# When the rows of x are loaded and Wq is turned: one fused attention and FFN kernel, its DMA queue reordered

## Chip, cores, metric

One core of a Trainium2 chip. The metric is the device time of one execution in microseconds (us), the median of several runs. The profiled span is some 1.7 us shorter than the time of the same execution. The experiments ran on three chips, each beside runs of the kernel before on the same chip in the same rounds; so medians of different rounds compare only roughly.

## The reference, cut to what matters

```python
x = A_x                                      # [1, 2048, 640], bf16
h  = x + _A_ref(_layernorm(x), A_wqkv, A_w_phi, A_wo)      # 32 heads of 20
h2 = h + _B_ref(_layernorm(h), B_w_gate, B_w_up, B_w_down) # (x Wg * x Wu) Wd, F = 1536
# _A_ref: q, k, v = x @ wqkv; phi(k) = [softmax(k w_phi), softmax(-k w_phi)], phi(q) likewise
#         kv = phi(k)^T v; num = phi(q) kv; den = phi(q) sum(phi(k)); out = (num / den) @ wo
```

## The kernel before

The 2048 rows are 16 tiles of 128. In the first third of the kernel each tile is loaded, normalised (VectorE statistics, then `xn`), turned so that the model dimension lies on the partitions (`xt`), and multiplied with Wv and Wk (`V`, `K`); `KV` sums phi(k)^T v. Tiles 0 to 3 are turned on TensorE, all others by a DMA transpose ("row turn") on the SyncE queue. The weights that make phi(q) are folded into Wq once (`F0`); for that Wq itself is turned by five DMA transposes (`wqt0` to `wqt4`), and the first fold needs all five.

All instructions are nodes of a graph. A table gives each a place, a list scheduler turns the places into one fixed order per engine, and each engine's program waits on semaphores only for what its next instruction needs. So every engine runs strictly in its order: an instruction that waits holds up all that stand behind it.

```python
xload("sp", 6, 8, -91, also=["act"])            # the last of the rows loaded with the weights
...
PACE = {t: [] for t in range(NT)}               # PACE[t]: issued only behind the row turn of tile t
...
for j in range(4):                              # x8, x10, x12, x14: two tiles of rows each
    PACE[3 + j].append(xload("sp", 8 + 2 * j, 10 + 2 * j, 10 * (3 + j) - 19))
for g in range(NC):                             # the five turns of Wq
    PACE[7 + g // 2].append(wqt(g, 10 * (7 + g // 2) - 19))
...
else:                                           # tiles 4 to 15: turned by DMA
    G.op("sp", "xt%d" % t, ... e.dma_start_transpose(out=T["xnT"][...], in_=T["xn"][...]), ...)
    for o_ in PACE[t]:
        o_.before.append(G.by["xt%d" % t])
```

The order of the SyncE queue that comes out: `w5 x0 x2 wk4 wv2 x6 x8 | xt6 xt4 x10 xt7 wqt0 x14 wqt1 xt5 x12 | xt8 wqt2 xt9 wqt4 wqt3 xt11 ...`. The ScalarE queue issues `x1 wk0 wk2 wv0 x4 wv4` (`wk2` is Wk's second piece: two row blocks, 320 KB).

The softmax here doesn't subtract the row's maximum and nothing guards it: scores larger than these inputs give would overflow.

Of the kernel before, what the change touches and what calls it, by code (L numbers as in the profile page):

```python
# [47 lines left out]
x0:1.18 wk0:1.18:1 wk2:1.66:1 wk4:2.14 x1:0.7 wv0:2.14 wv2:2.62:1 wv4:3.1 x2:1.66:1 x4:2.62:1 x6:3.1 w5:0.7 x8:3.58 x10:20.107 x12:25.947 x14:23.027  # L48
wqt0:21.807 wqt1:23.507 wqt2:31.138 wqt3:34.798 wqt4:33.578 wo0:51.868 wo2:49.468 wg0:49.948 wu0:52.348 wg1:52.828 wu1:50.428 wg2:50.908 wu2:51.388
wg3:48.988 wu3:47.548 wg4:48.028 wu4:48.508 id0:1.97 gl0:1.72 eps:0.7 id1:3.81 gla0:3.59 glb0:4.21 gla4:2.49 glb4:5.105 gla1:2.27 glb1:3.15 gla2:2.71  # L50
glb2:3.37 gla3:2.93 glb3:4.885 va1:0.9 glx:6.134 kv1:6.534 zero:0.7 warm0:1.08 warm1:1.51 warm2:1.94 warm3:2.37 warm4:2.8 warm5:3.23 warm6:3.66
warm7:4.09 warm8:4.52 warm9:5.019 Ph0:4.58:1 Ph1:4.43 Ph2:5.475 WT0:4.74 WTe0:5.289 WT1:5.239 WTe1:6.377 WT2:7.119 WTe2:7.807:1 WT3:6.84 WTe3:7.389
WT4:10.022 WTe4:10.572 F1_0:6.284 Fe1_0:6.869:1 F1_1:7.398 Fe1_1:8.022 F1_2:8.406 Fe1_2:9.269:1 F1_3:7.987 Fe1_3:8.646 F1_4:11.405 Fe1_4:11.99:1
L1s0:5.557 L1a0:6.795 L1s1:3.027 L1a1:4.027 L1s2:9.552 L1a2:10.552 L1s3:8.732 L1a3:10.372 L1s4:10.708 L1a4:12.848 L1s5:11.528 L1a5:14.708 L1s6:12.958
L1a6:14.598 L1s7:13.778 L1a7:14.818 L1s8:16.167 L1a8:24.428 L1s9:15.347 L1a9:22.078 L1s10:23.608 L1a10:25.358 L1s11:24.538 L1a11:26.888 L1s12:33.398
L1a12:36.248 L1s13:31.158 L1a13:34.718 L1s14:36.468 L1a14:37.468 L1s15:28.418 L1a15:36.358 L1l0:7.492 L1e0:7.922 L1l1:4.317 L1e1:4.747 L1l2:11.195
L1e2:11.625 L1n2:11.935 L1n3:12.135 L1l4:15.196 L1e4:16.04 L1n4:16.75 L1n5:16.55 L1n6:16.35 L1n7:16.95 L1l8:27.397 L1e8:27.857 L1n8:28.659 L1n9:28.859
L1n10:33.777 L1n11:33.977 L1l12:38.281 L1e12:38.711 L1n12:41.254 L1n13:41.454 L1n14:41.654 L1n15:41.854 xn0:8.232 xt0:9.127 xte0:9.892 xn1:5.057
xt1:5.737 xte1:6.905:1 xn2:12.348 xt2:13.901 xte2:14.573 xn3:12.613:1 xt3:13.621 xte3:14.928:1 xn4:17.487 xt4:18.887 xn5:17.387:1 xt5:24.727 xn6:16.987
xt6:17.667 xn7:19.407 xt7:20.587 xn8:29.238 xt8:29.918 xn9:29.462:1 xt9:32.358 xn10:34.218 xt10:37.238 xn11:34.91:1 xt11:36.018 xn12:41.988 xt12:42.668  # L60
xn13:42.488 xt13:45.108 xn14:42.378:1 xt14:43.888 xn15:44.408 xt15:46.328 V0_0:10.845 V0_1:11.117 V0_2:12.535 V0_3:12.806 V0_4:13.078 Ve0:13.95
K0_0:14.18 K0_1:14.451 K0_2:14.723 K0_3:14.995 K0_4:15.266 Kx0_0:16.14 Kx0_1:18.1 Ks0:19.907 Kr0:21.865 Ke0:22.728 Kn0:23.552 KV0:26.405 V1_0:9.479
V1_1:9.751 V1_2:11.72 V1_3:11.992 V1_4:12.263 Ve1:13.326 K1_0:7.713 K1_1:8.856 K1_2:10.302 K1_3:10.573 K1_4:13.35 Kx1_0:15.416 Kx1_1:16.763 Ks1:17.987
Kr1:19.97 Ke1:20.833 Kn1:21.193 KV1:29.798 V2:15.538 Ve2:19.347 K2:19.613 Kx2_0:21.242 Kx2_1:22.105 Ks2:25.468 Kr2:27.617 Ke2:28.067 Kn2:29.059
KV2:31.832 V3:18.255 Ve3:21.327:1 K3:16.896 Kx3_0:18.723 Kx3_1:20.21 Ks3:22.188 Kr3:24.958 Ke3:25.94 Kn3:26.3 KV3:33.866 V4:27.081 Ve4:28.838 K4:23.688
Kx4_0:25.317 Kx4_1:26.15 Ks4:26.998 Kr4:28.598 Ke4:30.798 Kn4:31.418 KV4:37.259 V5:32.508 Ve5:34.136 K5:28.439 Kx5_0:30.175 Kx5_1:31.008 Ks5:31.978
Kr5:33.688 Ke5:34.76 Kn5:36.536 KV5:40.967 V6:22.33 Ve6:24.335 K6:20.972 Kx6_0:22.878 Kx6_1:23.712 Ks6:29.738 Kr6:31.632 Ke6:32.082 Kn6:34.177
KV6:41.643 V7:25.047 Ve7:26.773 K7:30.474 Kx7_0:32.232 Kx7_1:33.065 Ks7:34.828 Kr7:36.794 Ke7:38.501 Kn7:38.895 KV7:46.709 V8:35.901 Ve8:37.657
K8:34.542 Kx8_0:36.171 Kx8_1:37.034 Ks8:37.867 Kr8:39.467 Ke8:39.917 Kn8:42.054 KV8:48.743 V9:37.935 Ve9:39.563:1 K9:39.293 Kx9_0:40.922 Kx9_1:41.755
Ks9:42.988 Kr9:44.885 Ke9:45.335 Kn9:45.695 KV9:50.777 V10:42.634 Ve10:44.262 K10:43.992 Kx10_0:45.62 Kx10_1:46.454 Ks10:47.287 Kr10:48.887 Ke10:49.75  # L70
Kn10:50.11 KV10:54.17 V11:56.205 Ve11:58.045 K11:45.35 Kx11_0:47.077 Kx11_1:47.91 Ks11:48.744 Kr11:50.584 Ke11:51.034 Kn11:52.469 KV11:60.28 V12:49.419
Ve12:51.184 K12:47.385 Kx12_0:49.127 Kx12_1:49.96 Ks12:50.794 Kr12:52.394 Ke12:52.844 Kn12:54.828 KV12:61.271 V13:54.846 Ve13:56.588 K13:51.453
Kx13_0:53.082 Kx13_1:53.915 Ks13:54.748 Kr13:56.348 Ke13:57.212 Kn13:57.572 KV13:62.262 V14:58.922 Ve14:60.648 K14:52.812 Kx14_0:54.538 Kx14_1:55.372
Ks14:56.205 Kr14:57.805 Ke14:58.668 Kn14:59.931 KV14:62.938 V15:63.929 Ve15:65.557 K15:57.563 Kx15_0:59.192 Kx15_1:60.025 Ks15:60.858 Kr15:62.458
Ke15:62.908 Kn15:63.268 KV15:67.446 KVe0:68.392 KVe1:69.612 KVe2:69.002 F0_0:42.319 Fe0_0:43.092 F0_1:60.956 Fe0_1:61.541 F0_2:63.614 Fe0_2:64.199
F0_3:40.652 Fe0_3:41.237:1 F0_4:61.947 Fe0_4:62.532:1 Q0_0:66.366 Qx0_0_0:68.232 Qx0_0_1:67.716 Q0_1:68.122 Qx0_1_0:69.471 Qx0_1_1:69.987 Q0_2:70.28
Qx0_2_0:71.629 Qx0_2_1:72.146 Q0_3:65.287 Qx0_3_0:67.153 Qx0_3_1:66.636 Q0_4:69.201 Qx0_4_0:70.55 Qx0_4_1:71.067 Q1_0:90.865 Qx1_0_0:92.214
Qx1_0_1:92.731 Q1_1:82.062 Qx1_1_0:83.412 Qx1_1_1:83.928 Q1_2:85.579 Qx1_2_0:86.928 Qx1_2_1:87.445 Q1_3:80.638 Qx1_3_0:82.504 Qx1_3_1:81.987
Q1_4:79.559 Qx1_4_0:80.908 Qx1_4_1:81.425 Q2_0:72.783 Qx2_0_0:74.649 Qx2_0_1:74.132 Q2_1:89.441 Qx2_1_0:90.79 Qx2_1_1:91.307 Q2_2:71.359 Qx2_2_0:72.708
Qx2_2_1:73.225 Q2_3:74.552 Qx2_3_0:76.418 Qx2_3_1:75.902 Q2_4:88.017 Qx2_4_0:89.882 Qx2_4_1:89.366 Q3_0:76.711 Qx3_0_0:78.06 Qx3_0_1:78.577 Q3_1:83.142  # L80
Qx3_1_0:84.491 Qx3_1_1:85.007 Q3_2:78.48 Qx3_2_0:79.829 Qx3_2_1:80.346 Q3_3:91.944 Qx3_3_0:93.293 Qx3_3_1:93.81 Q3_4:75.632 Qx3_4_0:77.497
Qx3_4_1:76.981 wd0:94.253 wd1:94.733 wd2:93.773 wd3:93.293 N0_1:73.862 N0_0:74.207 sr0:74.477 rho0:74.967 A0:75.337 B0:76.367 dd0:77.397 rd0:77.787
o0:78.267 oT0:79.688 O0:84.221 h0:86.057 L2s0:87.108 L2a0:88.108 L2v0:88.559 L2r0:90.778 hc0:89.038:1 hT0:89.929 N1_1:77.79 N1_0:72.438 sr1:78.405
rho1:78.895 A1:79.265 B1:80.295 dd1:81.325 rd1:81.715 o1:82.195:1 oT1:83.107 O1:86.658 h1:88.287 L2s1:89.538 L2a1:90.668 L2v1:90.958 L2r1:91.648
hc1:90.958:1 hT1:91.638 N2_1:89.096 N2_0:90.52 sr2:90.358 rho2:91.458 A2:91.828 B2:92.858 dd2:93.888 rd2:94.278 o2:94.758 oT2:96.179 O2:103.403
h2:105.032 L2s2:105.993 L2a2:107.423 L2v2:108.564 L2r2:109.277 hc2:107.713 hT2:108.637 N3_1:81.717 N3_0:78.135 sr3:82.927 rho3:83.417 A3:83.787
B3:84.817 dd3:85.847 rd3:86.808 o3:87.288 oT3:88.709 O3:93.023 h3:94.652 L2s3:95.713 L2a3:96.723 L2v3:97.013 L2r3:97.753 hc3:97.883:1 hT3:98.563
N4_1:94.382 N4_0:94.727 sr4:95.403 rho4:96.533 A4:96.903 B4:98.383 dd4:99.585 rd4:100.147 o4:100.798:1 oT4:101.71 O4:109.818 h4:111.822 L2s4:112.925
L2a4:114.055 L2v4:114.345 L2r4:115.455 hc4:114.345 hT4:115.268 N5_1:106.198 N5_0:104.762 sr5:107.113 rho5:107.885 A5:108.427 B5:109.758 dd5:110.96
rd5:111.522 o5:112.002 oT5:113.423 O5:116.563 h5:118.192 L2s5:119.123 L2a5:120.123 L2v5:120.413 L2r5:120.913 hc5:120.413:1 hT5:121.093 N6_1:99.984  # L90
N6_0:100.329 sr6:101.53 rho6:102.355 A6:102.933 B6:104.135 dd6:105.783 rd6:106.813 o6:107.293 oT6:109.857 O6:121.182 h6:122.81 L2s6:123.872
L2a6:124.882 L2v6:125.172 L2r6:128.373 hc6:125.172 hT6:126.095 N7_1:135.035 N7_0:141.855 sr7:135.65 rho7:142.47 A7:142.84 B7:143.87 dd7:144.9
rd7:145.29 o7:145.77 oT7:147.191 O7:151.868 h7:153.525 L2s7:154.457 L2a7:156.028 L2v7:156.318 L2r7:157.528 hc7:157.028:1 hT7:157.708 N8_1:112.958
# [131 lines left out]
def build_graph():  # L225
# [73 lines left out]
    PACE = {t: [] for t in range(NT)}  # L299
# [9 lines left out]
    for j in range(4):  # L309
        PACE[3 + j].append(xload("sp", 8 + 2 * j, 10 + 2 * j, 10 * (3 + j) - 19))  # L310
    for g in range(NC):
        PACE[7 + g // 2].append(wqt(g, 10 * (7 + g // 2) - 19))
# [720 lines left out]
```

## Time and profile before

| | before |
|---|---|
| time, median of the first 3 runs | 283.86 us (283.71 to 284.03) |
| profiled span | 282.4 us (that execution took 284.15 us) |
| TensorE busy | 275.9 us (98%) |
| VectorE, ScalarE, GpSimd busy | 62%, 38%, 23% |
| TensorE waits named in the profile | 3.2 us, of which 1.2 at the start |

How to read it: TensorE is the bound, so it is its own waits that can be won back, and as its program runs in order, a wait there delays all that follows. These lines of the page's DMA part (kernel before; size of one, then the median time from issue to landing) are the yardstick for the rest:

```profile
x_all<-in_A_x_dram SPq DMA_DIRECT2D x6, 320.0 KB, 5.2
xnT<-xn SPq DMA_TRANSPOSE x28, 2.6
scratch<-in_A_wqkv_dram SPq DMA_TRANSPOSE x5, 3.4
```

A row turn in a quiet queue takes 2.6 us to land. The prediction below shows the waits, the chain and the SyncE queue of the kernel before.

### The profile page before, as it was taken

The numbers are of one execution on the slowest core, as the hardware profiler recorded it, in microseconds if no ns is written. First come the engines' busy times: TensorE is split into PE (matmuls) and PEld (weight loads), VectorE is DVE, ScalarE is ACT, GpSimd is POOL, SyncE is SP. The second block draws the span as 40 slices with busy tenths as digits, with TensorE's granted clock in tenths as the row PEclk, the third lists the DMA queues.
The fourth block names the chain that finished last, engine by engine and source line by source line (L and its number), as shares of the span: only waits on it lengthen the run. The fifth ranks groups of instructions, "written<-read, shape, count | busy, mean of one in ns | idle before, by whom it ended". The sixth has DMA issues, their size and how long they took to land.

```text
span 282.4 us, 5039 instructions
## 1 busy us (share of the span) xinstructions
PE 275.9 (98%) x2060; PEld 183.1 (65%) x2075; DVE 175.7 (62%) x355; ACT 108.7 (38%) x215; POOL 65.7 (23%) x82
## 2 busy tenths in 40 slices
PE   8999899999999999999999999999999999999996
PEld 3777678777555688774455775546564655677874
DVE  4999886552387888886357857638533564723242
ACT  3898777776885632204231002131411112001310
POOL 7018898794012202222002201300001000000000
PEclk9999999999999999999999999999999999999999
DMA  7729543891031692632101241110501101021001
GB/s 223 247 39 190 123 94 72 251 401 50 0 26 24 154 234 49 80 93 48 25 0 26 44 98 46 23 23 2 95 3 46 46 0 49 0 71 47 0 11 61
DMA packets 43479, 21.98 MB, mean 78 GB/s; under 512 B 34624, under 2 KB 42176, under 8 KB 43456
## 3 DMA queue, kind: packets, MB, share of 16 engines
q1 hardware_dynamic: 42080, 20.02, 30.0%
q10 hardware_dynamic: 1376, 1.64, 1.8%
q8 instruction: 16, 0.26, 0.4%
q14 instruction: 7, 0.06, 0.1%
HBM read 11.00 MB, written 2.62 MB: 48 GB/s over the span
## 4 chain that ended last, share of the span: by engine, by line
PE 90%; DMA 7%; SPq 1%; issue 0%; ACTq 0%; ACT 0%; DVE 0%; DVEq 0%
PE ps L652 34%; PE ps L671 18%; PE ps L473 14%; PE ps L534 8%; PE ps L610 7%; PE ps L513 4%; PE ps L567 4%; DMA scratch<-scratch 3%; DMA scratch<-in_A_wqkv_dram 2%; DMA xnT<-xn 2%; PE ps L389 1%; SPq L274 1%; PE ps L370 0%; PE ps L451 0%; ACTq L274 0%
## 5 line engine op out<-in xcount | busy, mean ns | idle before, releaser
L652 PE MATMUL ps<-xnT,Wgu 128*128 128x512 bf16 (+1 forms) x589 | 106.1, 336 | 0.6
L652 PEld LDWEIGHTS ps<-xnT,Wgu 128*128 128x128 bf16 x600 | 58.2, 98 | 41.3 <-DVE ev L660 0.4
L657 ACT ACTIVATE scratch<-ps 128x512 bf16<-128x512 f32 (+1 forms) x60 | 30.7, 511 | 117.2 <-PE ps L652 111.3
L660 DVE TENSOR_TENSOR ev<-ps,scratch 128x512 bf16<-128x512 f32 (+1 forms) x60 | 33.2, 578 | 37.0 <-ACT scratch L657 21.6
L671 PE MATMUL ps<-Wp,ev 128*128 128x320 bf16 (+2 forms) x396 | 54.0, 295 | 0.0
L473 PE MATMUL ps<-Wp,xnT 128*128 128x320 bf16 x320 | 46.4, 299 | 1.1 <-DMA xnT<-xn 1.1
L671 PEld LDWEIGHTS ps<-Wp,ev 128*128 128x128 bf16 x396 | 38.1, 98 | 14.3
L504 POOL TENSOR_TENSOR ev<-ev,SR 128x1280 bf16<-128x1280 bf16 x16 | 37.5, 2356 | 10.0 <-ACT SR L502 10.0
L473 PEld LDWEIGHTS ps<-Wp,xnT 128*128 128x128 bf16 x320 | 30.5, 98 | 12.4 <-DMA xnT<-xn 1.4
L599 POOL TENSOR_TENSOR scratch<-scratch,sm 128x640 bf16<-128x640 f32 x13 | 16.5, 1270 | 91.7 <-DVE sm L596 91.4
L683 DVE SCALAR_TENSOR_TENSOR Wp<-ps,rs,x_all 128x640 bf16<-128x640 f32 (+3 forms) x18 | 14.5, 809 | 27.4 <-PE ps L671 27.3
L497 DVE TENSOR_REDUCE SR<-ev 128x64 f32<-128x1280 bf16 x16 | 23.4, 1472 | 10.3 <-ACT ev L494 10.3
L610 PE MATMUL ps<-Wo,scratch 128*128 128x320 bf16 x160 | 24.0, 299 | 0.5 <-DMA scratch<-scratch 0.5
L543 ACT ACTIVATE eqT<-ps 128x512 bf16<-128x512 f32 x40 | 21.6, 594 | 6.6 <-PE ps L534 6.6
L494 ACT ACTIVATE ev<-ps 128x640 bf16<-128x640 f32 x32 | 21.5, 709 | 5.5 <-PE ps L473 5.4
L534 PE MATMUL ps<-xnT,Wp 128*128 128x512 bf16 x96 | 22.8, 379 | 0.2
L610 PEld LDWEIGHTS ps<-Wo,scratch 128*128 128x128 bf16 x160 | 15.5, 98 | 7.9 <-DMA scratch<-scratch 0.7
L624 POOL TENSOR_SCALAR ln<-mv 128x1 f32<-128x1 f32 x16 | 3.3, 209 | 67.9 <-DVE mv L623 61.3
L614 DVE TENSOR_TENSOR x_all<-ps,x_all 128x640 bf16<-128x640 f32 x16 | 13.1, 819 | 7.1 <-PE ps L610 7.0
L567 PEld LDWEIGHTS ps<-KVm,eqT 128*128 128x128 bf16 x192 | 13.0, 98 | 4.5
L534 PEld LDWEIGHTS ps<-xnT,Wp 128*128 128x128 bf16 x100 | 9.6, 98 | 9.7
L567 PE MATMUL ps<-KVm,eqT 128*128 128x154 bf16 (+1 forms) x192 | 15.7, 221 | 0.0
(59 smaller groups left out, 202.7 us busy)
## 6 DMA issues: line engine op xcount, KB each, us to landing
out_dram<-Wp SPq DMA_DIRECT2D x15, 160.0 KB, 1.8
x_all<-in_A_x_dram SPq DMA_DIRECT2D x6, 320.0 KB, 5.2
Wgu<-in_B_w_up_dram SPq DMA_DIRECT2D x5, 384.0 KB, 9.5
Wgu<-in_B_w_gate_dram SPq DMA_DIRECT2D x5, 384.0 KB, 9.1
Wp<-in_B_w_down_dram SPq DMA_DIRECT2D x4, 480.0 KB, 5.5
scratch<-in_A_wqkv_dram ACTq DMA_DIRECT2D x2, 320.0 KB, 5.0
Wo<-in_A_wo_dram SPq DMA_DIRECT2D x1, 480.0 KB, 7.0
xnT<-xn SPq DMA_TRANSPOSE x28, 2.6
```

Source lines behind the costliest of these rows:

```text
L473: ins = e.matmul(pb(b, hb)[:, 0:320], lhsT=T["xnT"][:, NC - 1 - c, P * t:P * (t + 1)], rhs=T["Wp"][:, kind, c, 320 * hb:320 * (hb + 1)], s ...
L494: G.op("act", "Kx%d_%d" % (t, s), lambda e, s=s, b=b, ek=ek: e.activation(out=T["ek"][:, ek.slots[0], s, :].rearrange("p (b n) -> p b n", ...
L497: G.op("dve", "Ks%d" % t, lambda e, ek=ek, sr=sr: e.tensor_reduce(out=T["SR"][:, sr.slots[0], 0, :], in_=T["ek"][:, ek.slots[0], :, :].rea ...
L504: G.op("pool", "Kn%d" % t, lambda e, ek=ek, sr=sr: e.tensor_tensor(out=T["ek"][:, ek.slots[0], :, :].rearrange("p s (h f) -> p (s h) f", f ...
L534: ins = e.matmul(pb(b)[:, 0:n], lhsT=T["Wp"][:, 0, i, P * c:P * (c + 1)], rhs=T["xnT"][:, NC - 1 - i, o0:o0 + n], start=(i == 0), stop=(i ...
L543: G.op("act", "Qx%d_%d_%d" % (q, c, s), lambda e, s=s, c=c, o0=o0, n=n, b=b: e.activation(out=T["eqT"][:, s, c, o0:o0 + n], in_=pb(b)[:, 0 ...
L567: ins = e.matmul(pb(b, y)[:, 22 * h0:22 * (h0 + j1 - j0)], lhsT=T["eqT"][:, s, c, P * t:P * (t + 1)], rhs=T["KVm"][:, OFF[s, c] + j0:OFF[s ...
L610: ins = e.matmul(pb(b, hb)[:, 0:320], lhsT=T["oT"][:, oT.slots[0], c, :], rhs=T["Wo"][:, c, 320 * hb:320 * (hb + 1)], start=(c == 0), stop ...
L652: ins = e.matmul(pb(b)[:, 0:n], lhsT=T["Wgu"][:, gu, c, P * ft:P * (ft + 1)], rhs=T["xnT"][:, NC - 1 - c, o0:o0 + n], start=(c == 0), stop ...
L657: G.op("act", "g%d_%d" % (bi, ft), lambda e, pg=pg, gt=gt, n=n: e.activation(out=T["gt"][:, gt.slots[0], 0:n], in_=pb(pg)[:, 0:n], func=AF ...
L660: o_ = G.op("dve", "u%d_%d" % (bi, ft), lambda e, pu=pu, gt=gt, hh=hh, ft=ft, n=n: e.tensor_tensor(out=T["hh"][:, hh.slots[0], ft, 0:n], i ...
L671: ins = e.matmul(pb(b, hb)[:, 0:w], lhsT=T["hh"][:, hh.slots[0], ft, P * tt:P * (tt + 1)], rhs=T["Wd"][:, ft, c0 + w * hb:c0 + w * (hb + 1 ...
```

## The change

The intent: take the loads of x and the turns of Wq out of the queue's busy stretch at 20 to 30 us. The rows of x go where the DMA engines are still streaming weights, Wq's turns go behind the row turns of tiles 8 to 12. All places in the table are new; among 1013 entries, 24 put their instruction on another engine.

```diff
 for _t in """
-x0:1.18 ... x8:3.58 x10:20.107 x12:25.947 x14:23.027
-wqt0:21.807 wqt1:23.507 wqt2:31.138 wqt3:34.798 wqt4:33.578 ...
+... x8:5.02 x10:4.06 x12:4.54 x14:3.58
+wqt0:31.317 wqt1:33.907 wqt2:43.667 wqt3:37.567 wqt4:42.447 ...
 (the places of the other instructions: cut)
     for j in range(4):
-        PACE[3 + j].append(xload("sp", 8 + 2 * j, 10 + 2 * j, 10 * (3 + j) - 19))
+        xload("sp", 8 + 2 * j, 10 + 2 * j, 10 * (3 + j) - 19, also=["act"])
     for g in range(NC):
-        PACE[7 + g // 2].append(wqt(g, 10 * (7 + g // 2) - 19))
+        PACE[8 + g].append(wqt(g, 10 * (8 + g) - 19))
```

The SyncE queue becomes `w5 x0 x2 wk4 wv2 x6 x14 x10 x12 x8 | xt6 xt5 xt4 xt7 | xt8 wqt0 xt9 wqt1 xt10 xt11 wqt3 xt14 xt13 xt12 wqt4 wqt2 xt15 ...`.

## The prediction

> **What bounds the kernel now.** I read the page's head first, then the waits of TensorE, the chain of waits, the issues of the SyncE queue and last the stretches of 5 us. The head:
>
> ```profile
> span 282.4 us, 5039 instructions
> PE 275.9 (98%) x2060; PEld 183.1 (65%) x2075; DVE 175.7 (62%) x355; ACT 108.7 (38%) x215; POOL 65.7 (23%) x82
> PEclk9999999999999999999999999999999999999999
> ```
>
> TensorE is busy for 275.9 of 282.4 us at full clock, so all its idle time together is 6.5 us, 2.3% of the span. The change alters no matmul, so only those 6.5 us can shrink. The list of TensorE's waits says what they are:
>
> ```profile
> PE ps L349 <- DVE zero L344: 1.2, 1, 1.2
> PE ps L473 <- DMA xnT<-xn: 1.1, 1, 1.1
> PE ps L610 <- DMA scratch<-scratch: 0.5, 1, 0.5
> PE ps L370 <- DMA scratch<-in_A_wqkv_dram: 0.4, 1, 0.4
> ```
>
> The reader is to see four waits, 3.2 us in all; the rest of the 6.5 is the tail after the last matmul (about 2.5 us: the last one ends at 279.9) and crumbs. The first is the start of the program; the fourth is Wk's second piece, a load issued at 1.74 us. Neither is touched. The third lies near 106 us. Only the second lies in the part that the change is about, and the chain shows how it arises:
>
> ```profile
> 15.23 10.44 PE ps L473 x77
> 25.68 4.88 DMA xnT<-xn
> 30.60 1.53 PE ps L473 x10
> ```
>
> The turn (DMA transpose) of tile 5 is issued at 25.68 and lands after 4.88 us, at 30.6; K of tile 5 waits for it. The SyncE queue before that moment:
>
> ```profile
> 18.00 2.62 SPq L460 DMA_TRANSPOSE xnT<-xn  x2
> 20.67 0.58 SPq L274 DMA_DIRECT2D x_all<-in_A_x_dram  x1
> 21.29 1.21 SPq L460 DMA_TRANSPOSE xnT<-xn  x1
> 22.54 1.27 SPq L302 DMA_TRANSPOSE scratch<-in_A_wqkv_dram  x1
> 23.85 0.58 SPq L274 DMA_DIRECT2D x_all<-in_A_x_dram  x1
> 24.48 1.16 SPq L302 DMA_TRANSPOSE scratch<-in_A_wqkv_dram  x1
> 25.68 1.28 SPq L460 DMA_TRANSPOSE xnT<-xn  x1
> ```
>
> Ahead of tile 5's turn stand two x loads of 320 KB and two turns of Wq (L302). They cost it twice: it is issued late (SyncE spends 0.58 us on a load and about 1.27 us on a turn), and it shares the DMA engines. A row turn with no such neighbours lands in 2.6 us (page, the median of 28), this one in 4.88. The stretches agree:
>
> ```profile
> 5.00:10.00 5.00, 4.59 (x56) 3.65 (x56) 4.01 (x10) 2.85 (x6) 0.91 (x3) 1.00 1.04 369
> 10.00:15.00 5.00, 5.00 (x53) 3.90 (x51) 5.00 (x16) 4.68 (x10) 0.50 (x2) 1.00 0.39 129
> 15.00:20.00 5.00, 5.00 (x42) 3.63 (x40) 5.00 (x13) 5.00 (x11) 0.97 (x4) 1.00 0.15 29
> 25.00:30.00 5.00, 4.50 (x41) 3.22 (x38) 4.74 (x10) 4.02 (x12) 4.32 (x5) 1.00 1.00 203
> ```
>
> The last two columns are the DMA share and GB/s. DMA is nearly empty at 13 to 18 us and full at 25 to 30, exactly where TensorE (second number) falls from 5.00 to 4.50.
>
> **The Trainium skill.** "DMA: Bandwidth & Descriptors", section "Queues, rings and completion order", says that on each DMA engine descriptors are consumed in ring order, and that each engine goes round between the queues that have work. The trace agrees with the first: the SyncE queue's loads land in their order of issue, tile 6 at 12.4 and tile 8 at 13.2. It matters for the second: the last ScalarE-queue load (Wv's last piece, issued at 3.30) lands after 8.8 us, at 12.1, while the SyncE queue still has work, so one more load behind it should not take a larger share from it. Section "Issuing engines are not separate DMA queues" says that loads of all engines interleave on the same 16 engines; so moving a load earlier helps only if the engines are idle there, which the stretches show. "Perfetto Trace Analysis", "Per-instruction lifecycle", says that a DMA row in a profile ends when its descriptors are made and the movement lies outside it; the 1.28 us row with its landing after 4.88 us is such a case, so I go by landings.
>
> **The change part by part.**
> (1) The x loads of tiles 10, 12 and 14 move from 20.67, 23.85 and 27.00 us to right behind the load of tile 6, in the order 14, 10, 12, 8. Tile 8's load was already there: its pacing hung on tile 3, which is turned on TensorE and releases nothing late. So three loads move, 3 x 320 KB = 983 KB. Until 12.4 us nothing changes in the queue, and tile 14 takes the place of tile 8, landing at 13.2. At the 369 GB/s of the fullest stretch the other three take 0.89 us each: 10 at 14.1, 12 at 15.0, 8 at 15.8 (an estimate). The first row turns are issued at 18.00, so no overlap. The earliest reader is the statistics of tile 11 on VectorE, which the new order puts about where those of tile 9 stood (15.8 us before): about 1 us of room.
> (2) Wq's five turns move behind the row turns of tiles 8 to 12. Between 18.0 and 30 us the SyncE queue then has only the turns of 6, 5, 4, 7. At 1.31 us each they start at 18.0, 19.3, 20.6, 21.9 and land 2.65 us later: 20.7, 22.0, 23.3, 24.6. Readers: tile 6's at the place it had; V of tile 5 one projection ahead of V of tile 7; V7 has as many groups before it as before and starts at 25.9 (27.30, where the next group starts, less 1.36 for one projection); K4 at 27.3. The least room is 1.3 us. **The wait of 1.1 us goes.**
> (3) The price stands later: Wq's folding needs all five turns. The new order has twelve turns in a row from tile 8's on, the last of Wq's being the twelfth: 30.43 (tile 8's turn before) + 11 x 1.31 = 44.8, landing 3.0 to 3.4 us later, at 48.2. The first Wq fold in the new TensorE order comes 13 projections and 8 KV groups after the start of V7: 25.9 + 13 x 1.36 + 8 x 0.68 = 49.0. Room 0.8 us: no wait, but the tightest place I found.
> (4) The new order moves FFN pieces, puts some copies on other engines (24 of 1013 entries), and leaves the amount of work and the matmuls the same. TensorE ran all but gapless under the old order and I expect the same: 0.
> (5) The wait of 0.5 us at 106 us: the turn of tile 2's attention output stands behind the four Wd loads issued from 95.59 on, and lands 10.8 us after that. Loads, turn and reader all slide forward together by 1.1 us in the new order, so it stays.
> Sum: 283.86 - 1.1 = 282.8 us, with nothing added.
>
> **The rivals.**
> A. *The wait only moves*: the first fold waits for Wq's last turn, or a turn behind Wq's is late for its projection. For: room of only 0.8 us, and a turn of Wq landed after up to 4.1 us in the old trace. Against: that one had an x load beside it, which the new order lacks; the undisturbed ones took 2.8 to 3.4. It would give back 0.3 to 1.1 us: 283.1 to 283.9.
> B. *The early loads crowd the weights*: if Wv's last pieces or the rows of tiles 4 to 7 landed later because more is queued, projections at 12 to 15 us would wait. For: DMA share 1.04 at 5 to 10 us. Against: the added loads stand last in their ring. If all 983 KB went ahead, 2.7 us: up to 286.5.
> C. *The new order opens fresh waits after 70 us*, since some 200 us are rearranged and evacuations of VectorE and ScalarE have changed places. For: TensorE is in order, so each late evacuation is paid in full. Against: the old order had one such wait, of 0.5. I allow 0 to 1.5 us.
> D. *The wait at 106 us goes as well*: 282.3.
>
> **Range and chances.** The centre is the sum, 282.8, with C and D about cancelling. Below, waits two and three both gone and the runs' spread of 0.3 us give 282.1. Above, A in full or a middling C give 284.1. Faster by 2% would need 278.2 us, below the 275.9 of TensorE plus start and tail with hardly anything over, so 1%. Slower by 2% needs 5.7 us of new waits: 2%. Within: 97%.
>
> **What would show it.** In the changed profile: no TensorE wait for a row turn at L473; x loads all issued before 8 us and landed by about 16; row turns of tiles 4 to 7 landing after about 2.6 us each; DMA share near zero at 20 to 30 us; TensorE 5.00 of 5 in 25 to 30; the same 275.9 us of TensorE; the wait at L610 still about 0.5. Wrong if: a TensorE wait stands at L389 (the fold) or at L473 before 16 us, or several waits on VectorE or ScalarE appear after 70 us.

## The result

The changed kernel took 282.69 us (median of 4 runs, 282.39 to 282.86) against 283.78 us (4 runs, 283.44 to 284.03) for the kernel before. The ratio is 0.9961, 95% interval 0.9944 to 0.9979: the same at the 2% level, but faster by 0.4% and clear of zero. A ratio here is the mean time of one kernel's fast runs over the mean of the other's of the same rounds, so not quite the ratio of the medians quoted.

The head of the page of the changed kernel, and its TensorE waits (what waited, for whom: us in total, times, longest):

```profile
span 281.1 us, 5047 instructions
PE 274.9 (98%) x2058; PEld 182.7 (65%) x2075; DVE 176.8 (63%) x357; ACT 109.6 (39%) x217; POOL 61.3 (22%) x78
```

```profile
PE ps L370 <- DMA scratch<-in_A_wqkv_dram: 1.4, 2, 1.1
PE ps L349 <- DVE zero L344: 1.2, 1, 1.2
```

Of the four waits before, the one for tile 5's row turn (1.1 us) is gone, the one near 106 us (0.5) is gone too, and the one for Wk's first two pieces has grown from 0.4 to 1.4 us. The SyncE queue of the changed kernel up to 33 us (start, length, what, how many) shows the new order, five loads in a row and then row turns only:

```profile
3.37 5.28 SPq L274 DMA_DIRECT2D x_all<-in_A_x_dram  x5
18.56 13.41 SPq L460 DMA_TRANSPOSE xnT<-xn  x5
32.01 1.27 SPq L302 DMA_TRANSPOSE scratch<-in_A_wqkv_dram  x1
```

The same stretches as in the prediction, changed kernel (the second number is TensorE's busy time, the last two are the DMA share and GB/s):

```profile
10.00:15.00 5.00, 5.00 (x54) 3.87 (x52) 5.00 (x16) 4.69 (x10) 0.51 (x2) 1.00 0.98 331
15.00:20.00 5.00, 5.00 (x42) 3.67 (x41) 5.00 (x15) 5.00 (x11) 0.97 (x4) 1.00 0.06 14
20.00:25.00 5.00, 5.00 (x39) 3.60 (x38) 5.00 (x8) 4.69 (x13) 2.13 (x1) 1.00 0.66 126
25.00:30.00 5.00, 5.00 (x39) 3.62 (x37) 5.00 (x11) 4.26 (x11) 5.00 (x4) 1.00 0.03 7
```

The 983 KB of rows now flow at 10 to 15 us (DMA share 0.98 instead of 0.39), the stretch of 25 to 30 us is empty (0.03 instead of 1.00), and TensorE is full there. The stretch of 20 to 25 us is not empty (0.66, against 0.75 before): the row turns themselves are on their way there. What the page alone cannot say: whether the two other changes, the wait near 106 us and Wk's wait, belong to the change at all. That, and which part of it took tile 5's wait away, is what the experiments are for.

### The profile page after: what moved, and what is told of

Its sections match the earlier page's. It is cut to its first block, busy times and chain, and to the rows that moved or that the text cites. A ratio compares the mean times of both kernels' runs of the same rounds, so it can differ in the third digit from the quotient of the medians.

```text
span 281.1 us, 5047 instructions
## 1 busy us (share of the span) xinstructions
PE 274.9 (98%) x2058; PEld 182.7 (65%) x2075; DVE 176.8 (63%) x357; ACT 109.6 (39%) x217; POOL 61.3 (22%) x78
## 4 chain that ended last, share of the span: by engine, by line
PE 95%; DMA 2%; DVE 1%; issue 0%; ACTq 0%; ACT 0%; POOL 0%; DVEq 0%
PE ps L652 36%; PE ps L671 19%; PE ps L473 16%; PE ps L610 8%; PE ps L534 8%; PE ps L567 4%; PE ps L513 4%; DMA scratch<-in_A_wqkv_dram 2%; PE ps L389 1%; PE ps L370 0%; PE ps L451 0%; DVE x_all L614 0%; DVE ev L660 0%; DVE st L620 0%; ACTq L274 0%
## 5 line engine op out<-in xcount | busy, mean ns | idle before, releaser
L599 POOL TENSOR_TENSOR scratch<-scratch,sm 128x640 bf16<-128x640 f32 x10 | 12.7, 1273 | 94.9 <-DVE sm L596 91.7
L534 PE MATMUL ps<-xnT,Wp 128*128 128x512 bf16 x96 | 21.9, 379 | 0.2
```

Of the source, the lines that this page charges most:

```text
L534: ins = e.matmul(pb(b)[:, 0:n], lhsT=T["Wp"][:, 0, i, P * c:P * (c + 1)], rhs=T["xnT"][:, NC - 1 - i, o0:o0 + n], start=(i == 0), stop=(i ...
```

## The experiments

Twelve runs were made, all correct; those called again or look repeat a kernel unaltered. In those named e_ nothing but the places of a few DMA issues in the SyncE queue differs from the kernel before: the edit comes after the scheduler and touches the list of that queue alone. The helper used:

```python
def move(G, order, names, after):        # put DMA issues right behind another op of the queue
    L = order["sp"]
    mv = [G.by[n] for n in names]
    for o in mv:
        L.remove(o)
    k = L.index(G.by[after])
    lo, hi = L[k].start, L[k + 1].start
    for j, o in enumerate(mv):
        o.start = lo + (hi - lo) * (j + 1) / (len(mv) + 1)
    L[k + 1:k + 1] = mv
```

### b_again, a_again: both kernels once more

No edit.

> The kernel before, unaltered, timed against itself: how far a second profile and a second timing wander. Ratio 1.000, interval within 0.002 of it. If the wait for Wk's second piece (0.4 us before, 1.4 us in the changed kernel) is a matter of the run and not of the kernel, it should come out different from 0.4 here, anywhere in 0.3 to 1.5; if the early loads cause it, it stays near 0.4. The waits of 1.1 us for tile 5's turn and of 0.5 us before the output projection near 106 us stay if the order causes them.

> The changed kernel, unaltered. Ratio 0.996 (0.9955 to 0.997). If the early loads cause the longer wait for Wk's second piece, it is again 1.2 to 1.5 us; if it is a matter of the run, it may come out near 0.4. No wait for a row turn at L473, and if the order removed the wait near 106 us, none there.

Measured: b_again 284.22 us (282.74 to 285.00), ratio 1.0004 (0.9974 to 1.0035). a_again 282.63 us (282.19 to 282.98), ratio 0.9954 (0.9929 to 0.9978). TensorE waits (the 1.2 us at the start, `L349`, stands in every profile and is left out from here on), first of b_again:

```profile
PE ps L473 <- DMA xnT<-xn: 1.9, 1, 1.9
PE ps L370 <- DMA scratch<-in_A_wqkv_dram: 0.5, 1, 0.5
```

then of a_again:

```profile
PE ps L370 <- DMA scratch<-in_A_wqkv_dram: 1.3, 2, 1.0
```

Two things follow. The wait near 106 us is absent from this profile of the *old* kernel: its going is not to be booked to the change. And tile 5's wait is not a constant of 1.1 us, it was 1.9 here; the kernel before spreads over 2.3 us where the changed one spreads over 0.8. In the later rounds single runs of the kernel before, classed fast, took 286.32 and 286.97 us; such runs make the ratios of those rounds look better. The longer wait for Wk came back in a_again, so it looked like a matter of the kernel.

### e_loads: only the x loads early

```diff
         order, _ = schedule(G)
+        move(G, order, ["x14", "x10", "x12"], "x8")
```

> The kernel before with the three x loads alone issued early (tiles 14, 10, 12 behind tile 8); Wq's two turns still stand ahead of tile 5's. My theory, that either part alone is enough: tile 5's turn is issued about 1.2 us sooner (near 24.5) and lands in 2.7 to 3.5 us, the wait of 1.1 us goes, time 1.1 to 1.3 us less than before (ratio 0.996). Rival, that Wq's turns are the cause: landing still over 4 us, at least half of the wait stays, ratio 0.998 or more. If early loads crowd the weights, the wait for Wk's second piece is 1.2 us or more and the net gain is near 0.3 us.

Measured: 282.92 us (282.58 to 284.51), ratio 0.9984 (0.9951 to 1.0016). The waits of its profiled run (282.75 us):

```profile
PE ps L370 <- DMA scratch<-in_A_wqkv_dram: 0.7, 2, 0.4
PE ps L610 <- DMA scratch<-scratch: 0.3, 1, 0.3
```

Tile 5's turn was issued at 24.69 us and landed after 3.2 us, at 27.9; the wait is gone although both turns of Wq still stand ahead of it. Yet two of the six runs took 284.2 and 284.5 us, so by the times alone this part is not clear of zero. What those two runs waited for was not profiled.

### e_turns, e_turns2: only Wq's turns later

```diff
         order, _ = schedule(G)
+        move(G, order, ["wqt0", "wqt1"], "xt5")
```

> The kernel before with Wq's first two turns alone put behind tile 5's turn; x loads paced as before. My theory: tile 5's turn is issued near 23.2 and lands by 27.5, before its reader at 29.3, the wait of 1.1 us goes, ratio 0.996, and the wait for Wk's second piece is whatever b_again shows. Rival, that the x loads are the cause: the turn still lands 4 us or more after its issue, but being issued 2.5 us sooner it would be in time all the same; so only a wait of over 0.3 us left at K of tile 5 speaks against me. The wait near 106 us stays at about 0.5 in both.

> The same kernel as e_turns, whose profiled run fell into a state in which each 320-column matmul took 0.37 us; wanted is an undisturbed profile. Expected: no wait for tile 5's turn (issued near 23.2, landed by 27.5), the wait for Wk's second piece 0.4 to 0.5 as in the kernel before, the wait near 106 us 0 to 0.6. If instead over 0.3 us of waiting is left at K of tile 5, the x loads alone were the cause.

Measured: e_turns 282.89 us over all six runs, ratio of the fast ones 0.9971 (0.9936 to 1.0006); its profiled run took 751.22 us and is not compared (see the last section), the other five 282.16 to 284.76. The repeat, e_turns2: 282.52 us (282.01 to 282.65), ratio 0.9938 (0.9888 to 0.9988). Waits of e_turns2:

```profile
PE ps L370 <- DMA scratch<-in_A_wqkv_dram: 0.9, 1, 0.9
```

Tile 5's turn was issued at 23.48 us and landed after 4.0 us, at 27.5, still beside an x load and a turn of Wq. That is quicker than the 4.9 to 5.6 us of the kernel before, but far from the 2.6 of a quiet queue, and it was early enough for its reader at 29.3; even 5.6 us would have ended at 29.1. So being issued sooner was sufficient here; the landing need not become as quick as in a quiet queue. And Wk's wait was 0.9 us here, in the old order without early loads, against 0.4 expected: my expectation missed.

### e_both: both moves, nothing else

```diff
         order, _ = schedule(G)
+        move(G, order, ["x14", "x10", "x12"], "x8")
+        move(G, order, ["wqt0", "wqt1"], "xt5")
```

> The kernel before with both moves and no other change of order: three x loads early, Wq's first two turns behind tile 5's. Theory: each move alone already removes the whole wait, so together they bring no more than e_loads: 282.7 us, ratio 0.995 to 0.998; and the new order adds little, so this is within 0.3 us of the changed kernel. Rival, that the new order does much of the work: this stays 0.7 us or more above the changed kernel.

Measured: 282.76 us (282.20 to 283.18), ratio 0.9949 (0.9914 to 0.9985), within 0.1 us of the changed kernel's median in other rounds (its ratios: 0.9961 and, in a_again, 0.9954). Its waits:

```profile
PE ps L370 <- DMA scratch<-in_A_wqkv_dram: 0.4, 1, 0.4
```

So the two moves on the old order give all that the whole change gives. The thousand other places that were rewritten with it brought nothing on top that these runs can see.

### a_wait: are the early loads to blame for Wk's wait?

```diff
         order, _ = schedule(G)
+        for k, t in enumerate((14, 10, 12, 8)):
+            G.by["x%d" % t].start = 8.0 + 0.5 * k       # same place in the queue
+        G.by["x14"].alldeps[G.by["WT2"]] = True         # wait for the turn of Wk's second piece
```

> The changed kernel with the last four x loads held back until Wk's second piece has been turned on TensorE (near 8.5 us), in the same place of the queue. If issuing them at 4 to 8 us slows the loads ahead of them, Wk's second piece now lands by 7.9 instead of 8.3 and its wait falls from 1.3 to 0.4-0.6 us; no row is late, since the queue ahead is not empty before 12.3; time 282.0 (0.7 less than the changed kernel). If the longer wait has another cause, it stays at 1.3 and the time at 282.7.

Measured: 282.50 us (282.30 to 282.86), ratio 0.9943 (0.9909 to 0.9977). The four loads were issued at 8.94 to 10.38 us instead of 4 to 7, and still landed by 16.2. Wk's wait:

```profile
PE ps L370 <- DMA scratch<-in_A_wqkv_dram: 1.1, 2, 0.7
```

Wk's second piece landed at 8.13 us, against 8.37 and 8.30 in the two profiles of the changed kernel. The expected drop to 0.4-0.6 us did not come (the three profiles of the changed kernel have 1.3 to 1.6), and e_both had the early loads with a wait of only 0.4. So my theory falls: issuing more loads behind Wk is not what makes this wait longer.

### a_wqlast: how much room has the fold of Wq?

```diff
         order, _ = schedule(G)
+        move(G, order, ["wqt2"], "xt15")
```

> The changed kernel with the last turn of Wq put behind that of tile 15, one turn later. It tests how much room the first fold of Wq has: in the changed kernel the turn landed at 49.35 and the fold began at 49.60. If that room is real, a turn later by 1.3 us makes the fold wait 0.9 to 1.2 us and the time 283.6. If the fold has slack that I do not see, the time stays at 282.7.

Measured: 283.32 us (283.05 to 283.50), ratio 0.9970 (0.9928 to 1.0013). TensorE around the first fold (L389), changed kernel first, then a_wqlast (start, length, what; in brackets the idle time before):

```profile
48.92 0.84 PE L513 MATMUL ps<-ev 128*128 128x147 bf16 x12
49.60 0.48 PE L389 MATMUL ps<-Phi,scratch 128*128 128x140 bf16 x6
```

```profile
48.76 0.84 PE L513 MATMUL ps<-ev 128*128 128x147 bf16 x12
50.33 0.48 PE L389 MATMUL ps<-Phi,scratch 128*128 128x140 bf16 x6 [0.72 <-ACT SR L502]
```

The turn was issued one turn later and landed at 50.1 us; the fold started 0.2 us after that. The profile puts the wait down to ScalarE, but only the turn was moved and it landed just before the fold, so the wait is the DMA's. The room in the changed kernel, 49.35 (landing) to 49.60 (fold), is real and is a quarter of a microsecond. The wait (0.7 us) and the time came out below the 0.9 to 1.2 us and 283.6 us expected.

### b_look2, b_look3, a_look2: more profiles

No edit; one run each.

> A third profile of the kernel before. Expected: a wait at K of tile 5 of 0.5 to 2.5 us, its turn landing over 4 us after issue; the time of the run 281.8 us plus all TensorE waits but the one at the start, within 0.5. An instruction fetch of 16 KB falls between the turn's issue and landing, as in both earlier profiles. The wait near 106 us is 0 to 0.6, different from run to run.

> A fourth profile of the kernel before, for the spread: as for b_look2. If the wait at K of tile 5 differs by 0.5 us or more among the four while its turn is issued at the same time within 0.3 us, it is the DMA's landing that makes the times of this kernel spread.

> A third profile of the changed kernel. In four profiles of its order Wk's second piece landed at 8.13 to 8.37, in six of the old order at 7.51 to 8.11. If that is a property of the order, it lands again at 8.1 or later; if chance, anywhere in 7.5 to 8.4. No wait for a row turn, none near 106 us.

Measured: b_look2 283.09 us, b_look3 283.98 us, a_look2 282.81 us. Tile 5's wait in the four profiles of the kernel before was 1.1, 1.9, 1.2 and 1.9 us (before, b_again, b_look2, b_look3), its turn issued at 25.68, 25.60, 25.17 and 25.54 and landed after 4.9, 5.6, 5.0 and 5.5 us. Three of the four were issued within 0.14 us of each other (b_look2 0.4 us sooner) and still waited 1.1 to 1.9 us, so it is mostly the landing that varies. What goes with the long ones shows in the DMA queues of the stretch 27 to 30 us (packets, MB, share of the 16 engines' time). Before:

```profile
q1 hardware_dynamic: 1111, 0.51, 97.7%
q14 instruction: 1, 0.01, 0.7%
```

b_again:

```profile
q1 hardware_dynamic: 751, 0.28, 100.6%
q14 instruction: 1, 0.01, 3.9%
```

b_look2:

```profile
q14 instruction: 1, 0.01, 0.7%
```

b_look3:

```profile
q14 instruction: 1, 0.01, 3.9%
```

In the two profiles with 1.9 us of waiting, the single 8 KB instruction fetch of queue 14 took 3.9% of 16 engines times 3 us, which is 1.9 us; in the two with 1.1 and 1.2 it took 0.7%, 0.3 us. The Trainium skill ("DMA: Bandwidth & Descriptors", "Queues, rings and completion order") lists row 14 as the runtime's own, and says ("Why a DMA increments its semaphore by 16 and not by 1") that a DMA counts as landed only when each of its engines has written its increment. With that, one engine held up by a fetch holds up the whole turn. The four profiles fit, two and two; no run moved a fetch, so it is an association, not shown. There is a rival: in the same two profiles queue 1 was 100.6% busy and yet moved only 0.28 and 0.36 MB, against 0.51 (97.7%) and 0.44 MB (57.8%) in the others, so everything in that stretch was slow and the long fetch may be a symptom like the late turn.

The spans add up. The span less TensorE's listed waits, except the one at the start, is 279.4 to 280.4 us in all thirteen undisturbed profiles: 282.4 - 2.0 = 280.4 before, 281.1 - 1.4 = 279.7 changed, 282.3 - 2.9 = 279.4 in b_look3, and so on. That remainder varies by 1.0 us, nearly as much as the gain, and between profiles of one kernel; b_look2 and b_look3 had been expected at 281.8 us plus their waits, within 0.5, and both missed, 0.6 and 0.7 us lower. The variation lies at the start: the first ten transposes of Wk (L370) took 0.71 and 0.66 us per five before, 0.45 and 0.44 in b_look3. From the first fold of Wk (L389, begun at 6.6 to 7.3 us) to the end, less the waits listed after it, all thirteen take 273.1 to 273.5 us. Why TensorE is slow for longer at the start of some executions was not tried.

As for Wk's second piece: it landed at 7.0 to 8.1 us in seven undisturbed profiles of the old order, with early loads (e_loads 7.89, e_both 7.81) or without, and at 8.1 to 8.4 us in five of the new one (the nearest two, 8.11 and 8.13, almost touch). The wait for Wk averages 0.7 us in the old and 1.3 us in the new. In these twelve profiles it goes with the new order, not with the loads. The separation is thin: in a_wqlast the load was issued 0.15 us later than elsewhere, and counted from its issue it took 6.3 us, within the old order's 5.3 to 6.4. In the first 8 us the two orders differ only in the sequence of GpSimd's small set-up instructions and in one Phi product put on VectorE. Which of these matters, and how, was not tried and stays open.

### a_split: Wk's second piece in two halves

```diff
         order, _ = schedule(G)
+        # wk2 (ScalarE queue) loads row block 2 alone; wk3, new, loads block 3 on the SyncE queue behind x0
+        w3 = copy.copy(w2); w3.name, w3.eng, w3.alldeps = "wk3", "sp", {}
+        w2.emit, w3.emit = piece(2), piece(3)
+        order["sp"].insert(order["sp"].index(G.by["x0"]) + 1, w3)
+        G.by["WT3"].alldeps[w3] = G.by["WT3"].alldeps.pop(w2)
```

> The changed kernel with Wk's second piece (two row blocks, 320 KB, ScalarE queue) cut in two, the second half issued on the SyncE queue behind tile 0's row. It is the largest wait left in TensorE apart from the start. By the traffic of the traces (some 180 KB per us on each queue at 5 to 8 us) the two halves land near 7.0 and 6.3 instead of 8.1 to 8.4, so the wait of 0.7 to 1.1 us goes to 0 to 0.3; tile 2's rows land some 0.8 us later, at about 9.2, before their reader at 9.7 to 10.2. Expected 281.9 us, 0.7 less than the changed kernel. If the rows of tile 2 or Wk's last piece become the next wait, the gain is 0.3 or less.

Measured: 281.92 us (281.64 to 282.16), ratio 0.9906 (0.9857 to 0.9956), the fastest of all here; the kernel before had a median of 284.25 us in the same rounds and a_look2's single run 282.81. Its waits, and TensorE at the place of the old wait:

```profile
PE ps L370 <- DMA scratch<-in_A_wqkv_dram: 0.4, 1, 0.4
```

```profile
6.77 0.49 PE L389 MATMUL ps<-Phi,scratch 128*128 128x140 bf16 x6
7.10 0.72 PE L370 MATMUL ps<-ident,scratch 128*128 128x128 bf16 x10
```

In the changed kernel that L370 row starts at 8.41 us after 1.08 us of waiting. The halves landed at 5.92 and 6.38 us (7.0 and 6.3 expected), Wk's second wait is gone (the 0.4 us left is for the first piece), and the rows of tile 2, which gave way, landed at 8.53 us, in time. Against the changed kernel's 282.69 us, taken in other rounds, the gain is 0.8 us (0.7 expected); the wait of 1.1 us that is gone is the firmer evidence. Two things were changed at once: the load was halved, and its second half was put ahead of tile 2's rows. Which of them did it was not separated.

## Why the prediction was right

- **The sum**: 282.8 forecast, 282.69 measured, but two of its terms were off and cancelled.
- **Step 2, tile 5's wait goes**: right, and the mechanism too. The turns of tiles 6, 5, 4, 7 were issued at 18.56, 19.91, 21.21 and 22.54 and landed 2.7 us later. The forecast did not say that either part alone would do; e_loads and e_turns2 show it, in one profile each. The term was taken from one profile (1.1); over four it is 1.1 to 1.9, mean 1.5. That the total agreed within 0.1 us is in part luck.
- **Step 5, "so it stays"**: not borne out. The wait near 106 us was 0.5 us in one of four profiles of the kernel before, 0.3 in e_loads and absent in all others, changed or not. I had taken one profile's wait for a property of the order. Rival D, that it goes as well, is what the profile showed, but so did b_again, so it is not the change's doing as far as the runs show.
- **Rival B, crowded weights**: I weighed it as unlikely, and its symptom came: Wk's wait is 0.6 us longer on average. But e_both has the loads without the symptom and a_wait holds them back without removing it. It goes with the new order, which step 4 had put at 0; what in it is open.
- **Step 1**: the spacing was right (0.80 to 0.89 us a load, 0.89 forecast), the times 0.9 to 1.0 us early (tile 8 last at 16.76, not 15.8), since the load ahead of them was late already: "until 12.4 us nothing changes" did not hold. The rows of tiles 6 and 7 landed 10.0 us after their issue; 8.4 to 9.4 us in the five undisturbed profiles of runs without early loads, 9.2 to 10.0 in the six with them, 9.4 in a_wait. So early loads tend to delay the load before them by some tenths of a microsecond, the part of rival B that came true. No reader waited.
- **Step 3, the price**: right that the fold does not wait, and right that it is the tightest place. Its room was put at 0.8 us and is 0.25, since the row of twelve turns did not run without pauses (46.13 for the last instead of 44.8), while the fold came only 0.6 us later than forecast (49.60, not 49.0).
- **Step 4 and rival C**: after 70 us no wait of TensorE is listed in any undisturbed profile but that near 106 us.
- **Signs that did not come**: DMA share near zero from 20 to 30 us held for the second half only (0.66 and 0.03): the row turns alone keep it busy. TensorE busy was 274.9 us, not 275.9; as 17 matmul records are missing from that trace (2058, against 2075 in the fullest) and 15 from the one before, this decides nothing.

In terms of means: 1.5 us won at tile 5, 0.6 lost at Wk, and the wait near 106 us a matter of luck, leave about 0.9 of the 1.1 us measured. The rest is of the size by which the span less all waits differs between the four profiles of the kernel before (mean 279.9) and the three of the changed one (279.6).

## What to carry to other kernels

In a kernel whose TensorE runs without gaps, look for the few waits that end on a DMA, and see what stands ahead of that DMA in its queue: issuing it 1 to 2 us sooner was enough, even where it still took 4.0 us to land. Profile the unchanged kernel more than once before a wait of half a microsecond is booked as a property of the order; here three of four waits changed from run to run. The next wait was found by reading the same list again: a load that TensorE waits for, halved over two queues and with one half moved forward, was worth about another 0.8 us.

## What the Trainium skill lacked or had wrong

- "DMA: Bandwidth & Descriptors" names row 14 as runtime-internal but has no figure for what its fetches cost others. Here single 8 KB instruction fetches took 0.3 to 1.9 us, and TensorE waited 1.1 to 1.2 us for tile 5's turn with the short ones and 1.9 us with the long ones (an association, see above).
- The same page gives no time from issue to landing for a DMA transpose of a tile. Here one of 128 x 640 bf16 kept the SyncE queue for about 1.27 us and landed 2.6 to 2.7 us after its issue in a quiet queue, 3.2 to 5.6 us beside x loads or turns of Wq.
- Its rule ("Rules for kernel authors") that spreading DMAs over SyncE, ScalarE and GpSimd queues does not help bandwidth held for the total (372 GB/s at 5 to 10 us in a_split, 367 in the changed kernel). The rule does not speak of the order of arrival, which changed: Wk's second piece, halved over two queues with one half moved ahead, was complete at 6.38 instead of 8.37 us.
- "TensorE: Matmul & The Clock Gate", "Seeing it yourself", warns that clock events in a trace have been seen to be unreliable. The profiled run of e_turns may be such a case, for the whole program: below, the head of its page, and two projections (20 matmuls of 320 columns) in its timeline. They took 7.7 us, against 2.88 in the timelines of the other kernels, while VectorE and ScalarE were busy for as long as ever (179.3 and 109.7 us) and the run is listed with a granted clock of 1.00. (Its page lacks the line of the clock, but so does that of e_both, an ordinary run.) It occurred in one run; whether the clock was low is not shown, and the cause is open.

```profile
span 749.5 us, 5039 instructions
PE 740.6 (99%) x2060; PEld 341.1 (46%) x2075; DVE 179.3 (24%) x355; ACT 109.7 (15%) x215; POOL 65.9 (9%) x82
```

```profile
64.34 7.72 PE L473 MATMUL ps<-Wp,xnT 128*128 128x320 bf16 x20
```
